# The order in which VectorE walks the tail tokens when it scales them out of PSUM

## The chip, the cores and the metric

The kernel runs on one core of one Trainium2 chip. Times are device microseconds of one execution, as the chip reports them. A profile covers the span from the first to the last instruction, which is some 1.8 us shorter. PE is the matrix engine (PEld its weight loads), DVE is VectorE, ACT ScalarE, POOL GpSimd, and SP the engine that issues the transfers, all but five in the trace before. One run of the kernel before took 1665 us and is left out. The two kernels with a probe at their end (e4, e11) ran once each, at a mean granted TensorE clock of 0.98 and 0.96. Inside the kernel PE keeps the pace of the other traces in both (from 135.6 to 241.6 us their gain is 0.00 us in the table of the experiments), so its starts there can be compared; from the probes themselves only VectorE and ScalarE durations are taken. The rounds of experiments ran on different chips of one kind (the record lists chips 1, 3 and 6), each beside the kernel before on the same chip.

## The reference

Retention attention over 8 batches of 8 heads, 576 tokens and 64 dimensions, then a feed-forward pair with a tanh gelu:

```python
scores = scale * np.matmul(q, k.transpose(0, 1, 3, 2))
gamma = 1.0 - 2.0 ** (-5.0 - np.arange(H, dtype=np.float32))
Dmat = np.where(rel >= 0, gamma[:, None, None] ** rel[None, :, :], 0.0)
ret = np.matmul(scores * Dmat, v)                 # 8 x 8 x 576 x 64
x = ret.transpose(0, 2, 1, 3).reshape(4608, 512)
h = x @ w_in                                      # 512 -> 2048
g = 0.5 * h * (1.0 + np.tanh(c * (h + 0.044715 * h**3)))
out = g @ w_out                                   # 2048 -> 512
```

## The kernel before: what matters here

576 tokens are four chunks of 128 and a **tail** of 64. The tails of all 8 batches are gathered in one tile and go through the feed-forward layers together, as a block of their own near the end.

```python
xt = const.tile([128, 2, B, HP, 32], F16, name="xt")   # parity, batch, head pair, token / 2
...
def inter_tail(b):
    xs = att[b].pop("xt")                              # two PSUM banks
    for u in range(2):
        for s in range(2):
            nc.tensor.matmul(xs[u][:, 64 * s : 64 * s + 64], ...)          # L547
        nc.vector.tensor_tensor(                                           # L553
            out=xt[:, :, b, 2 * u : 2 * u + 2, :].rearrange("p s q i -> p q i s"),
            in0=xs[u][:, 0:128].rearrange("p (q i s) -> p q i s", q=2, s=2),
            in1=gx[:, 2 * u : 2 * u + 2, :, 0:32].rearrange("p q s i -> p q i s"),
            op=ALU.mult,
        )
```

The order of the instructions on every engine is fixed by a hand-made plan: around a matmul unit it lists which piece of the next batch's attention is issued behind it. The tail of batch 7 is followed by five additions into `xf` (L609), which read all of `xt`, and by the tail block's matmuls (L613), which read `xf`.

## Time and profile before

| | kernel before |
|---|---|
| time, four runs | 299.68 to 300.29 us, median 299.89 |
| span of the profile | 297.5 us |
| PE busy | 289.5 us |
| VectorE busy | 234.3 us |
| L553 | 16 instructions of 128 elements per partition, 838 ns each by their records, 0.60 us each in a queue |

A group's busy time is the union of its records. Records of neighbouring VectorE instructions overlap by about 0.09 us (L408: a mean record of 0.69 us, 0.60 us in the chain), more with slow ones (L553: 0.84 and 0.60). The cost of an instruction in a queue therefore has to be read from the chain or from the starts of those behind it. The lines themselves stand in the prediction.

### The profile page before, as it was taken

To read this page: it belongs to the slowest core of one execution; us is meant where nothing else is said; L and a number is where in the kernel's file an instruction comes from. 1 tells how busy PE (TensorE), PEld (TensorE's weight loads), DVE (VectorE), ACT (ScalarE), POOL (GpSimd) and SP (SyncE) were. 2 spreads that over 40 slices of the span, in tenths; PEclk is the share of its full clock that TensorE was granted. 3 is DMA by queue.
4 is the path that set the end of the run, shared out by engine and by line. 5 is a ranking of instruction groups with operands and counts; after the bars stand their busy time and mean duration, and the time that the engine had idled before them with its cause. 6 is when DMAs were issued, how large, how long until landed. Compare 5 with 4: busy or idle time off the path is not lost.

```text
span 297.5 us, 8910 instructions
## 1 busy us (share of the span) xinstructions
PE 289.5 (97%) x3748; PEld 208.9 (70%) x3748; DVE 234.3 (79%) x434; ACT 161.9 (54%) x316; POOL 121.6 (41%) x142
## 2 busy tenths in 40 slices
PE   8989999999999999999999999999999999999995
PEld 6866478888885568645875587558755876686584
DVE  2796889999998996898569746977698298886754
ACT  7328798975546781665446544555346217615720
POOL 6743676276140433183063206459003005711760
PEclk9999999999999999999999999999999999999999
DMA  6999999969879989988994989481120003002204
GB/s 203 301 312 324 311 374 331 266 175 223 227 199 219 315 217 207 292 252 130 260 278 115 135 240 280 127 145 18 61 84 0 2 0 145 0 2 71 71 3 141
DMA packets 94712, 52.48 MB, mean 176 GB/s; under 512 B 38352, under 2 KB 88528, under 8 KB 94672
## 3 DMA queue, kind: packets, MB, share of 16 engines
q1 hardware_dynamic: 94336, 51.26, 65.2%
q10 hardware_dynamic: 336, 0.66, 0.8%
q8 instruction: 29, 0.48, 0.6%
q14 instruction: 11, 0.09, 0.1%
HBM read 36.70 MB, written 9.44 MB: 155 GB/s over the span
## 4 chain that ended last, share of the span: by engine, by line
PE 74%; DVE 13%; DMA 4%; SPq 4%; issue 2%; ACT 2%; DVEq 0%; ACTq 0%
PE hp L583 27%; PE my L726 9%; PE mz L726 9%; PE hp L669 5%; PE mw L726 5%; PE mu L726 4%; PE mv L726 4%; SPq L188 3%; DVE ret L408 3%; DMA loan<-in_moe_w_in_dram 2%; DMA ld<-in_moe_w_in_dram 2%; PE xs L495 2%; DVE gT L698 2%; DVE ost L753 2%; PE xs L522 2%
## 5 line engine op out<-in xcount | busy, mean ns | idle before, releaser
L583 PE MATMUL hp<-x,w_in_sb 128*128 128x512 f16 x408 | 94.1, 379 | 0.2 <-DVE ret L408 0.2
L587 ACT ACTIVATE gT<-hp 128x512 f16<-128x512 f32 x112 | 65.9, 598 | 42.3 <-PE hp L583 40.4
L583 PEld LDWEIGHTS <-w_in_sb 128*128 128x128 f16 x448 | 42.5, 98 | 44.9 <-issue 0.8
L726 PEld LDWEIGHTS <-gT 128*128 128x128 f16 x576 | 55.8, 98 | 8.0
L241 POOL TENSOR_TENSOR cv<-ld,sc 128x512 f16<-128x512 f32 x28 | 31.4, 1136 | 28.8 <-DMA ld<-in_v_dram 26.0
L408 DVE TENSOR_TENSOR ret<-st,cm 128x512 f16<-128x512 f32 x64 | 40.8, 694 | 1.9 <-PE st L395 1.6
L232 POOL CAST kq<-ld 128x512 f16<-128x512 f32 x31 | 20.7, 677 | 51.8 <-DMA ld<-in_k_dram 26.3
L232 ACT CAST tbd<-ws 64x256 f16<-64x256 f32 x61 | 24.6, 403 | 24.7 <-DVE ws L476 21.3
L726 PE MATMUL my<-w_out_sb,gT 128*128 128x256 f16 x288 | 34.4, 273 | 0.0
L726 PE MATMUL mz<-w_out_sb,gT 128*128 128x256 f16 x288 | 34.4, 273 | 0.0
L726 PEld LDWEIGHTS <-gsum 128*128 128x128 f16 x288 | 28.1, 98 | 3.6
L698 DVE TENSOR_TENSOR gT<-gT 128x1024 f16<-128x1024 f16 x30 | 28.5, 955 | 0.2
L535 DVE TENSOR_TENSOR x<-xs,gx 128x512 f16<-128x512 f32 x32 | 21.6, 684 | 5.2 <-PE xs L522 5.0
L694 DVE TENSOR_TENSOR gsum<-gT 128x1024 f16<-128x1024 f16 x32 | 23.4, 730 | 2.7 <-ACT gT L656 2.7
L686 DVE TENSOR_TENSOR gdia<-gT 128x512 f16<-128x512 f16 (+1 forms) x30 | 22.5, 751 | 2.4 <-ACT gT L587 2.1
L753 DVE TENSOR_TENSOR ost<-ost,mv 128x512 f32<-128x512 f32 x18 | 11.5, 682 | 16.4 <-issue 11.5
L694 POOL TENSOR_TENSOR gsum<-gT 128x1024 f16<-128x1024 f16 x4 | 8.9, 2223 | 35.1 <-ACT gT L656 32.2
L669 PE MATMUL hp<-x,w_in_sb 128*128 128x256 f16 x160 | 19.1, 273 | 1.1 <-DVE x L535 0.9
L669 PEld LDWEIGHTS <-w_in_sb 128*128 128x128 f16 x160 | 15.2, 98 | 3.4 <-issue 1.0
L726 PE MATMUL mu<-w_out_sb,gsum 128*128 128x256 f16 x144 | 17.2, 272 | 0.3 <-issue 0.2
L726 PE MATMUL mw<-w_out_sb,gdia 128*128 128x256 f16 x144 | 17.2, 273 | 0.0
L726 PE MATMUL mv<-w_out_sb,gsum 128*128 128x256 f16 x144 | 17.2, 273 | 0.0
(114 smaller groups left out, 410.8 us busy)
## 6 DMA issues: line engine op xcount, KB each, us to landing
ld<-in_k_dram SPq DMA_DIRECT2D x30, 256.0 KB, 5.4
ld<-in_q_dram SPq DMA_DIRECT2D x30, 256.0 KB, 5.4
ld<-in_v_dram SPq DMA_DIRECT2D x30, 256.0 KB, 5.3
out_dram<-ost SPq DMA_DIRECT2D x14, 512.0 KB, 4.1
loan<-in_moe_w_out_dram SPq DMA_DIRECT2D x12, 256.0 KB, 5.7
loan<-in_moe_w_in_dram SPq DMA_DIRECT2D x8, 256.0 KB, 6.4
ld<-in_moe_w_in_dram SPq DMA_DIRECT2D x8, 256.0 KB, 6.2
ld<-in_moe_w_out_dram SPq DMA_DIRECT2D x4, 256.0 KB, 5.1
```

What stands on the lines that cost most here:

```text
L232: (eng.copy if eng is nc.scalar else eng.tensor_copy)(out=out, in_=in_)
L241: eng.tensor_tensor(out=unperm(att[b]["v"][:, s, hh, :]), in0=perm(t), in1=sc[:, 8 * hh : 8 * hh + 8] .rearrange("p (r h) -> p r h", r=2) ...
L408: nc.vector.tensor_tensor(out=x.rearrange("p (a m) -> p a m", a=2), in0=st[hl].rearrange("p (a m) -> p a m", a=2), in1=cm.rearrange("p r s ...
L535: nc.vector.tensor_tensor(out=xb[b][:, :, 2 * s + c].rearrange("p s q i -> p q s i"), in0=att[b]["x", s][c].rearrange("p (q s i) -> p q s ...
L583: nc.tensor.matmul(hp, w_in_sb[:, ct, 128 * f : 128 * f + 128], x[:, :, ct, :], start=(ct == 0), stop=(ct == 3),)
L587: nc.scalar.activation(out=self.g(f // 2)[:, f % 2], in_=hp, func=AF.Gelu_apprx_tanh)
L669: nc.tensor.matmul(hp[:, 256 * h : 256 * h + 256], w_in_sb[:, ct, 256 * j + 128 * h : 256 * j + 128 * h + 128], xb[self.b][:, :, 2 * u : 2 ...
L686: e.tensor_tensor(out=self.sa[:, j : j + n], in0=g[:, :, 0, 0:256], in1=g[:, :, 1, 256:512], op=ALU.add)
L694: e.tensor_tensor(out=self.sc[:, j : j + n], in0=g[:, :, 0], in1=g[:, :, 1], op=ALU.add)
L698: e.tensor_tensor(out=g.rearrange("p j h c -> p j (h c)")[:, :, 256:768].rearrange("p j (h c) -> p j h c", h=2), in0=g[:, :, :, 0:256], in ...
L726: nc.tensor.matmul(o, lhs(j, slice(128 * u, 128 * u + 128)), w_out_sb[:, j, w], start=((u == 0 or isinstance(t, list)) and j == 0 and not ...
L753: nc.vector.tensor_tensor(out=out, in0=in0, in1=t, op=op)
```

## The change

Intent: a row of the tile should be written in one go, not one element in this row and one in that. The innermost index becomes the token pair (i), and the parity (s) moves outside it. All values and places stay the same. The price is that the PSUM read, which was contiguous, now takes every second float.

```diff
-                out=xt[:, :, b, 2 * u : 2 * u + 2, :].rearrange("p s q i -> p q i s"),
-                in0=xs[u][:, 0:128].rearrange("p (q i s) -> p q i s", q=2, s=2),
-                in1=gx[:, 2 * u : 2 * u + 2, :, 0:32].rearrange("p q s i -> p q i s"),
+                out=xt[:, :, b, 2 * u : 2 * u + 2, :].rearrange("p s q i -> p q s i"),
+                in0=xs[u][:, 0:128].rearrange("p (q i s) -> p q s i", q=2, s=2),
+                in1=gx[:, 2 * u : 2 * u + 2, :, 0:32],
```

## The prediction

> **What bounds the kernel now.** I read the page's busy table first. The matrix engine is busy 97% of the span and VectorE, the only engine that the change touches, 79%.
>
> ```profile
> PE 289.5 (97%) x3748; PEld 208.9 (70%) x3748; DVE 234.3 (79%) x434; ACT 161.9 (54%) x316; POOL 121.6 (41%) x142
> ...
> PE   8989999999999999999999999999999999999995
> ...
> DVE  2796889999998996898569746977698298886754
> ```
>
> The second line is PE in 40 slices of 7.4 us: only the first slices and the last one are below nine tenths. So anything VectorE gives back can shorten the run only where PE stands still for it, and PE idles 8 us in all (297.5 - 289.5), most of it in the first 40 us and at the very end. VectorE, in contrast, is full in one stretch (slices 7 to 15, about 45 to 112 us) and has room later.
>
> The change touches one group, so I read the groups of VectorE by shape next. The columns after the bar are total busy us, mean ns of one, idle us before, and what ended that idle time.
>
> ```profile
> L408 DVE TENSOR_TENSOR ret<-st,cm 128x512 f16<-128x512 f32 x64 | 40.8, 694 | 1.9 <-PE st L395 1.6
> ...
> L535 DVE TENSOR_TENSOR x<-xs,gx 128x512 f16<-128x512 f32 x32 | 21.6, 684 | 5.2 <-PE xs L522 5.0
> ...
> L553 DVE TENSOR_TENSOR xt<-xs,gx 128x128 f16<-128x128 f32 x16 | 10.4, 838 | 6.0 <-PE xs L547 6.0
> ...
> L436 DVE TENSOR_TENSOR rett<-st,cm 128x128 f16<-128x128 f32 x16 | 3.8, 281 | 0.5 <-PE st L423 0.5
> ```
>
> L553 is the tail's scaling: 16 instructions (8 batches x 2), 128 elements per partition each. L436 has the same operation, shape, types and memories (one input in PSUM, fp16 result in SBUF) and takes 281 ns; L553 takes 838 ns, more than L535, which does the same job on four times the elements. What differs is only the walk. L553 goes "q i s", so its last index is the token's parity: each write jumps between two rows of the tile that lie 1024 fp16 elements apart (8 batches x 4 pairs x 32), and each read of gx jumps 64 floats; only its PSUM read is contiguous.
>
> Records of neighbouring VectorE instructions overlap, so a record overstates what one costs in a queue. The chain of waits (start, us, what) shows the cost in the queue:
>
> ```profile
> 72.72 0.40 DVE rett L436 x2
> ...
> 74.72 1.21 DVE xt L553 x2
> ...
> 81.05 1.21 DVE ret L408 x2
> 82.30 0.44 PE us L459 x30
> ```
>
> Two L436 cost 0.40 us, two L553 cost 1.21, exactly as much as two 512-element L408. So in a queue one L553 costs 0.60 us and a contiguous instruction of its size 0.20.
>
> [...] the new walk makes the PSUM read the one that steps: two floats at a time. No row of this trace shows such a read.
>
> **The change part by part.** It removes and adds no instruction: the orders before and after have the same rows on all engines, with only L553's pattern changed, from 128x64x2 to 128x2x2x32. The values and their places are the same.
> - Write: runs of 32 fp16 in place of a jump each element. The gx read: runs of 32 floats. [...]
> - PSUM read: contiguous before, every second float after. At best free: 0.20 us in a queue, like L436. [...] I take 0.27 us, a record of about 330 ns[...]; this is a choice[...].
> - Saving: 0.60 - 0.27 = 0.33 us each, 0.66 a pair, 5.3 us over the 16 instructions. VectorE's busy time falls from 234.3 to about 229 (227.9 if the read is free).
>
> That 5.3 us is not time off the kernel. xt is read only by the tail block from about 242 us on, so seven of the eight pairs have no reader near. Their one use of time is to hold up the VectorE instructions queued behind them. I therefore looked at each stretch behind a pair, for PE's starts that came later than the usual spacing (216 ns for 512 columns, 109 for 256). Behind the first pair (74.65 us) there are four places where PE waited for VectorE's queue:
>
> ```profile
> 82.04 0.70 PE L459 MATMUL us<-cv,kq 64*64 64x64 f16 x32
> ...
> 97.27 0.38 PE L352 MATMUL tr<-ident,kqt 128*128 128x128 f16 x4 [0.16 <-DVE vs L473]
> ...
> 132.88 0.38 PE L583 MATMUL hp<-x,w_in_sb 128*128 128x512 f16 x1 [0.23 <-DVE ret L408]
> ...
> 243.41 0.39 PE L613 MATMUL pw<-xf,wf 128*128 128x256 f16 x2 [0.16 <-DVE xf L609]
> ```
>
> - 82.3: about 0.25 us inside the us group and 0.35 before the mu product behind it; the chain runs back through VectorE, without idle time, to the pair at 74.7. At most 0.6; POOL's work on cv also starts at 82.05, so I count 0.3.
> - 97.3: 0.22 us late, the transposes wait for a bank that VectorE frees, right behind the pair at 95.3. I count 0.2.
> - 132.9: 0.39 us late, again behind an unbroken VectorE queue from the pair at 125.0. VectorE instructions between them also wait for ScalarE's results, so I count 0.25.
> - 243.4: 0.32 us late. Here the pair (240.55) is truly on the path: it feeds xf, and pw waits for xf. I count 0.3.
>
> Sum 1.05 us, at most 1.5. In the blocks from 155 to 230 us PE's chain is unbroken and most of the 6.0 us that VectorE idles ahead of L553 lie there; saving there is worth nothing. 300.0 - 1.05 gives 299.0; I take 299.1.
>
> **Rivals.**
> (a) Nothing moves at all: PE is 97% busy, and the VectorE time was hidden. Against it speak only the four small waits above. 299.8 to 300.2.
> (b) The PSUM read with a step turns out as slow as the old write: L553 stays near 800 ns and the time at 300.0. Against it: before, two streams jumped by far and one of them wrote half words[...].
> (c) VectorE's queue is tighter than I see in its full stretch (45 to 112 us) and every 0.66 us there carries through: three pairs, 2 us, plus 0.6 later: 297.4. Against it: PE's lateness in 74 to 112 us is too small in sum to give 2 us back.
> (d) Earlier VectorE frees banks earlier, so PE and transfers run into another wait, for instance POOL's cv at 82 us [...]. This would eat the gain: 300.0, perhaps 300.5.
>
> **Range and chances.** Runs of the kernel before spread over 0.5 us by themselves (299.78 to 300.29). With 1.05 us expected, 1.5 as the limit of the direct gain, and (a) and (d) together as likely as one in three, I put 8 in 10 on 298.3 to 300.1. Faster by 2% would mean 294, more than all of PE's idle time after 40 us; slower by 2% has no mechanism, as no work is added. Both get 0.01.
>
> **What would show it.** Right: L553's mean record falls to 280 to 480 ns (central 330) with the count still 16; two of them in the chain cost 0.4 to 0.8 us; VectorE's busy time falls by 4 to 6.5 us with PE's busy time within 1 us of 289.5; the waits at 97, 133 and 243 us shrink or go; VectorE's idle time ahead of other groups grows by about what L553 loses. Wrong: if L553 stays above 600 ns the step about the PSUM read fails; if it falls and the span doesn't, the four waits are held by something else than VectorE; if the span falls by over 2 us, PE was held up by VectorE in ways that its start times hide.

The sum of 1.05 us has its four terms (0.3, 0.2, 0.25 and 0.3), which come from the trace before. The 0.27 us in a queue was my choice: it lies above the 0.20 us of L436, and nothing measured then said by how much. On it rest 0.33 us for each instruction, 0.66 a pair and 5.3 in all. That the new walk's write and its read of gx would cost nothing more was not shown either when I counted so; e4_probe has the new walk and the all contiguous form both at 291 ns.

## The result, and the profile after

| | before | after |
|---|---|---|
| time, four runs each | 299.68 to 300.29, median 299.89 us | 298.07 to 298.73, median 298.46 us |
| ratio | | 0.995, 95% interval 0.9932 to 0.9967 |
| span of the profile | 297.5 us | 296.3 us |

Ratios are the mean time of one kernel's fast runs over that of the other's in the same rounds, so they are not quite the ratio of the medians. Two later comparisons on the same code (below) gave 0.997 and 0.9986.

First the busy times of the changed kernel, then two of its VectorE groups by shape, to be held against the same lines in the prediction:

```profile
PE 288.9 (97%) x3748; PEld 208.6 (70%) x3748; DVE 230.7 (78%) x434; ACT 162.0 (55%) x316; POOL 122.4 (41%) x142
```

```profile
L553 DVE TENSOR_TENSOR xt<-xs,gx 128x128 f16<-128x128 f32 x16 | 3.9, 284 | 6.0 <-PE xs L547 6.0
L436 DVE TENSOR_TENSOR rett<-st,cm 128x128 f16<-128x128 f32 x16 | 3.8, 281 | 1.2 <-PE st L423 1.2
```

L553 now looks like L436, the contiguous instruction of its size: 284 against 281 ns. The step in the PSUM read costs nothing. The chain of waits of the changed kernel says the same of the queue, 0.40 us a **pair** (the two instructions of a batch) where it was 1.21:

```profile
72.51 0.40 DVE rett L436 x2
...
74.52 0.40 DVE xt L553 x2
74.92 0.34 DVE vs L473
```

Read from the start of the second instruction behind a pair (near 125 us: 1.73 us after the pair's own start before, 1.00 now) the saving is 0.73 us a pair, a little less than the 0.81 of the chain.

L553's busy time fell by 6.5 us (10.4 to 3.9), but VectorE's by 3.6 (234.3 to 230.7). Of the missing 2.9 us, 2.3 are one other group, L694, which the change doesn't touch: 23.4 us before and 25.7 after. In four traces of kernels with the old walk in most places it is 24.6, 24.6, 25.1 and 25.8, so the first trace was low in it and the walk isn't the reason.

Where did PE get its time? All kernels here run the same 3748 matmuls in the same order. So the start of the n-th matmul in the trace before, minus the start of the n-th in another trace (each from its own span's start), is that trace's **lead**, and the growth of the lead within a stage is what was gained there. For the first trace of the changed kernel (stages named by the time in the trace before):

| stage | to 73.2 | 73.2 to 90.0 | 90.0 to 99.2 | 99.2 to 130.7 | 130.7 to 135.6 | 135.6 to 241.6 | 241.6 to 244.1 |
|---|---|---|---|---|---|---|---|
| gain, us | 0.37 | 0.64 | -0.39 | -0.17 | 0.39 | 0.00 | 0.33 |

The first changed instruction runs at 74 us, so 0.37 us of the lead cannot come from the change. The loss at 90 to 99 us is a new wait. In the timeline of the changed kernel, PE (columns: start, us, engine, line, operation, tiles, and in brackets its idle time and who ended it) stands before the scores of batch 3:

```profile
95.84 0.86 PE L395 MATMUL st<-T 64*64 64x128 f16 x48 [0.70 <-DMA T<-kq]
```

It waits for the transposing DMA that fills T. The loss of 0.17 us at 99 to 131 us comes back in no other trace either. The gain at 243 us is the place where `xf` waits for the last pair. First the kernel before, then the changed one, same columns:

```profile
240.55 1.28 DVE L553 TENSOR_TENSOR xt<-xs,gx 128x128 f16<-128x128 f32 x2
...
242.28 1.75 DVE L609 TENSOR_TENSOR xf<-xt 128x512 f16<-128x512 f16 x5
...
242.65 0.60 PE L613 MATMUL pv<-xt,wf 128*128 128x256 f16 x4
```

```profile
239.71 0.48 DVE L553 TENSOR_TENSOR xt<-xs,gx 128x128 f16<-128x128 f32 x2
...
240.27 0.69 DVE L753 TENSOR_TENSOR ost<-ost,my 128x512 f32<-128x512 f32 x1
...
240.87 1.76 DVE L609 TENSOR_TENSOR xf<-xt 128x512 f16<-128x512 f16 x5
...
241.81 0.60 PE L613 MATMUL pv<-xt,wf 128*128 128x256 f16 x4
...
242.25 0.38 PE L613 MATMUL pw<-xf,wf 128*128 128x256 f16 x2
```

Before, `xf` started 0.37 us ahead of pv and pw waited for it (0.16 us of idle PE in the prediction's line at 243.41). Now it starts 0.94 us ahead of pv, and pw follows pv with no wait in brackets.

So three questions were open: is it the time in VectorE's queue that counts, and where; does the change bring the wait for the transpose; and which of the old walk's streams was slow?

### The profile page after: what moved, and what is told of

It reads as the page before. It is cut to its first block, busy times and chain, and to the rows that moved or that the text cites. A ratio compares the mean times of both kernels' runs of the same rounds, so it can differ in the third digit from the quotient of the medians.

```text
span 296.3 us, 8910 instructions
## 1 busy us (share of the span) xinstructions
PE 288.9 (97%) x3748; PEld 208.6 (70%) x3748; DVE 230.7 (78%) x434; ACT 162.0 (55%) x316; POOL 122.4 (41%) x142
## 4 chain that ended last, share of the span: by engine, by line
PE 78%; DVE 13%; DMA 4%; ACT 2%; issue 1%; SPq 0%; POOL 0%; DVEq 0%; ACTq 0%
PE hp L583 31%; PE my L726 9%; PE mz L726 9%; PE mw L726 5%; PE mu L726 4%; PE mv L726 4%; PE hp L669 3%; DMA T<-kq 3%; DVE ret L408 3%; PE st L395 2%; PE xs L495 2%; PE py L613 2%; DVE ost L753 2%; PE xs L522 2%; DVE x L535 1%
## 5 line engine op out<-in xcount | busy, mean ns | idle before, releaser
L587 ACT ACTIVATE gT<-hp 128x512 f16<-128x512 f32 x112 | 65.8, 598 | 41.9 <-PE hp L583 40.1
L232 POOL CAST kq<-ld 128x512 f16<-128x512 f32 x31 | 22.0, 716 | 57.7 <-DMA ld<-in_k_dram 42.3
L241 POOL TENSOR_TENSOR cv<-ld,sc 128x512 f16<-128x512 f32 x28 | 32.8, 1184 | 28.4 <-DMA ld<-in_v_dram 23.8
L408 DVE TENSOR_TENSOR ret<-st,cm 128x512 f16<-128x512 f32 x64 | 40.0, 681 | 4.2 <-PE st L395 3.9
L232 ACT CAST tbd<-ws 64x256 f16<-64x256 f32 x61 | 24.6, 403 | 22.5 <-DVE ws L476 21.9
L694 DVE TENSOR_TENSOR gsum<-gT 128x1024 f16<-128x1024 f16 x32 | 25.7, 802 | 2.7 <-ACT gT L656 2.7
L535 DVE TENSOR_TENSOR x<-xs,gx 128x512 f16<-128x512 f32 x32 | 21.5, 683 | 4.8 <-PE xs L522 4.6
L686 DVE TENSOR_TENSOR gdia<-gT 128x512 f16<-128x512 f16 (+1 forms) x30 | 21.9, 731 | 2.8 <-ACT gT L587 2.1
L694 POOL TENSOR_TENSOR gsum<-gT 128x1024 f16<-128x1024 f16 x4 | 8.9, 2222 | 34.8 <-ACT gT L656 31.8
```

The lines of the kernel that those rows point to most:

```text
L232: (eng.copy if eng is nc.scalar else eng.tensor_copy)(out=out, in_=in_)
L241: eng.tensor_tensor(out=unperm(att[b]["v"][:, s, hh, :]), in0=perm(t), in1=sc[:, 8 * hh : 8 * hh + 8] .rearrange("p (r h) -> p r h", r=2) ...
L408: nc.vector.tensor_tensor(out=x.rearrange("p (a m) -> p a m", a=2), in0=st[hl].rearrange("p (a m) -> p a m", a=2), in1=cm.rearrange("p r s ...
L535: nc.vector.tensor_tensor(out=xb[b][:, :, 2 * s + c].rearrange("p s q i -> p q s i"), in0=att[b]["x", s][c].rearrange("p (q s i) -> p q s ...
L587: nc.scalar.activation(out=self.g(f // 2)[:, f % 2], in_=hp, func=AF.Gelu_apprx_tanh)
L686: e.tensor_tensor(out=self.sa[:, j : j + n], in0=g[:, :, 0, 0:256], in1=g[:, :, 1, 256:512], op=ALU.add)
```

## The experiments

**Theory.** The old walk's 2-byte writes cost 0.40 us an instruction, and PE gets back only what VectorE's queue made it wait for. **Rivals.** The scattered writes hurt other engines at the SBUF; every pair's saving counts alike; the wait for the transpose belongs to the change; or the waits of PE that the prediction listed are held by something else.

Some edits add a line ahead of the scaling, so its number is L554 in their profiles, and those behind it move by one as well.

The stage gains of all traces but two (e3 and e10, below) over the first trace of before, in us, worked out as above:

| trace | pairs with the new walk | to 73.2 | 73.2-90.0 | 90.0-99.2 | 130.7-135.6 | 135.6-241.6 | 241.6-244.1 |
|---|---|---|---|---|---|---|---|
| changed kernel | all | 0.37 | 0.64 | -0.39 | 0.39 | 0.00 | 0.33 |
| e1_again | all | -0.05 | 0.53 | 0.00 | 0.39 | -0.06 | 0.33 |
| e12_once_more | all | -0.04 | 0.47 | 0.00 | 0.39 | -0.07 | 0.33 |
| e4_probe | all | -1.62 | 0.72 | -0.01 | 0.39 | 0.00 | 0.33 |
| e11_distance | all | 0.01 | 0.27 | 0.00 | 0.39 | 0.00 | 0.33 |
| e5_first3 | batches 0 to 2 | 0.34 | 0.40 | 0.00 | 0.39 | 0.00 | 0.00 |
| e6_mid | batch 3 | -0.09 | -0.15 | 0.00 | 0.39 | 0.00 | 0.00 |
| e7_456 | batches 4 to 6 | -0.57 | -0.16 | 0.00 | 0.39 | 0.00 | 0.00 |
| e8_last | batch 7 | -0.66 | -0.59 | 0.00 | 0.38 | 0.00 | 0.33 |
| e9_twice | all, each issued twice | 0.09 | -0.26 | 0.03 | 0.14 | 0.00 | 0.07 |
| e2_thrice | all, each issued three times | -0.53 | -0.58 | -0.28 | 0.39 | 0.00 | -0.58 |

The column to 73.2 us is the spread that an execution brings before any changed instruction runs. It is as large as the whole effect, which is why the stages are compared and not the spans.

### e1_again and e12_once_more: the changed kernel twice more

Edit: none.

> The changed kernel once more, unaltered, for more rounds and a second trace. Both theories: ratio to the kernel before 0.994 to 0.996. The point is the trace: in the first one PE waited 0.86 us at 95.8 us for the transposing DMA into T, a wait the kernel before did not have. If the change brings that wait (rival: the earlier PE runs into the transfer), it is there again at 0.3 us or more; if it comes from where the transfers stood in that one execution (they were 0.9 us late before the first changed instruction ran), it need not be.

> The changed kernel a third time, because the two timed comparisons gave 0.995 and 0.997. From the traces so far the gain is 0.4 to 0.7 us in the stretch 73 to 90 us over kernels with the old walk there (which lost 0.2 us on average against the first trace of before), and 0.33 us at 243 us: about 1.05 us, ratio 0.9965 with the interval holding it. In the trace: time from the matmul at 73.2 us to the last one 219.2 to 219.8 us, no gain at 97 us and none from 136 to 241 us. Rival (the first result of 1.4 us was the size): ratio 0.995 or less.

Measured: 0.997 (interval 0.9948 to 0.9991) and 0.9986 (0.996 to 1.0013). The first of them missed the ratio that I had named. The second lies above 0.9965 too; its interval holds that, but also 1.000. The first result of 0.995 thus lies at the favourable end. **The wait for the transpose** is gone from PE in both, and in the two probe traces of the same code: their gain at 90 to 99 us is zero within 0.01. In the first trace the transpose was issued at 87.13 us, against 86.20 in the trace before, and PE came there a us earlier. The queue of transfers had been late by 0.9 us before the first changed instruction ran (70.80 for 69.86), had caught up to 0.1 us at 74.35, and fell back again by 77. So it varies from one execution to the next, and the wait is no fixed cost of the change. The 0.86 us of the expectation is the length of that group of matmuls; the wait in the first trace is the 0.70 us in brackets. An earlier PE does have less room in front of that transfer, and one of five traces used it up. Whether it would do so more often than before, five traces can't tell.

### e5_first3, e6_mid, e7_456, e8_last: one part of the change alone

```diff
+            w = "p q s i" if b < 3 else "p q i s"     # b == 3; b in (4, 5, 6); b == 7
-                out=xt[...].rearrange("p s q i -> p q s i"),
+                out=xt[...].rearrange("p s q i -> " + w),   # in0 and in1 likewise
```

> Old walk but for batches 0 to 2 (the pairs near 74.7, 91 and 95 us). Theory: what VectorE's full stretch holds of the gain, 0.3 to 0.9 us, ratio 0.997 to 0.999; the waits of PE near 132.9 and 243.4 us stay. Rival (one late wait carries the whole gain): ratio 0.9995 to 1.001.

> New walk for batch 3 alone (the pair near 125 us). Theory: PE's lateness of 0.39 us at 132.9 us goes and PE's lead behind it is 0.3 to 0.4 us more than in front of it, and nothing else changes: ratio 0.9985 to 0.9995. Rival: the wait there is held by the gelu results or by POOL and stays: ratio 1.000.

> New walk for batches 4 to 6 alone. Theory: nothing, ratio 0.9995 to 1.0005, PE's lead from 150 to 240 us unchanged within 0.1 us, though VectorE is busy 1.2 us less there in each batch pair's 0.8 us. Rival (each pair's saving counts alike): 3 of 8 of the gain, ratio 0.998.

> New walk for batch 7 alone (the pair near 240.5 us, the one that xf waits for). Theory: PE's lateness of 0.32 us at 243.4 us goes: ratio 0.9985 to 0.9993, lead of PE 0.3 us more behind 243.4 than in front. Rival: the wait moves to another instruction of VectorE ahead of xf: ratio 1.000.

Measured: ratios 0.9997 (0.9969 to 1.0025), 0.9982 (0.996 to 1.0004), 0.9987 (0.9967 to 1.0007) and 0.9984 (0.9959 to 1.001). All four intervals hold 1.000, and all four ratios lie outside the ranges that I had named: parts of 0.3 to 0.7 us are too small for the times, and only the traces separate them.

- **First three batches:** 0.40 us at 73 to 90 us, where the three traces with the old walk in all of these pairs, taken on the same chip, have -0.15, -0.16 and -0.59. All of it comes before 90 us, ahead of the second and third pair (near 91 and 95 us). So of the three only the first pair counts. It counts at two places. One is the wait near 82.3 us that the prediction listed. The other, which it did not list, is at 78 us: in the kernel before, the second half of a group of scores starts at 78.09 us, behind VectorE's L535, which ended at 78.04 us. The group takes 0.83 us there, 1.01 in e8_last (old walk) and 0.64 in e1_again (new walk); one line of each, in this order:

```profile
77.68 0.83 PE L395 MATMUL st<-T 64*64 64x128 f16 x32
...
78.33 1.01 PE L395 MATMUL st<-T 64*64 64x128 f16 x32
...
77.72 0.64 PE L395 MATMUL st<-T 64*64 64x128 f16 x32
```

- **The third pair** brings nothing, for VectorE then waits for ScalarE. Its next instruction starts 1.19 us after the pair's start with the old walk and with the new one; with the new walk VectorE stands idle for 0.70 us in front of it (the changed kernel):

```profile
95.45 0.43 DVE L686 TENSOR_TENSOR gdia<-gT 128x512 f16<-128x512 f16 x1 [0.70 <-ACT gT L587]
```

- **Batch 3:** PE's lateness at 132.9 us is gone, as expected. But it is gone in e5, e7 and e8 too, whose batch 3 has the old walk, and in e2, whose pair there costs more than the old one. So the gain of 0.39 us at 131 to 136 us isn't the change's: the one trace of the kernel before was late there. What made it late I did not settle.
- **Batches 4 to 6:** nothing between 136 and 242 us, as expected, though each pair is 0.8 us cheaper.
- **Batch 7:** 0.33 us at 243 us, as expected, and in no trace with the old walk there. The line behind the first stage's loss in this trace is the same wait as in the kernel before, for VectorE's scaled scores behind the old first pair:

```profile
83.43 0.44 PE L459 MATMUL us<-cv,kq 64*64 64x64 f16 x30 [0.34 <-DVE ret L408]
...
84.02 0.71 PE L727 MATMUL mu<-w_out_sb,gsum 128*128 128x256 f16 x5 [0.16 <-DVE ret L408]
```

### e2_thrice and e9_twice: the new walk at the old price

```diff
+            for _ in range(3):        # e9: range(2)
                 nc.vector.tensor_tensor(out=xt[...], in0=..., in1=...)   # the new walk
```

> The new walk, but each of the 16 scalings issued three times in a row: three times 0.20 us is the 0.60 us that one cost with the old walk. Theory (only the time in VectorE's queue counts): back to the kernel before within 0.2%, ratio 0.998 to 1.002, lead of PE near 0. Rival (the scattered writes themselves hurt the other engines that read or write SBUF): the gain stays, ratio 0.994 to 0.997.

> The dose of the thrice run was too high: its pairs cost 1.69 us in the queue, not 1.21, since repeats on one tile cost 0.28 us each. Here each scaling of the new walk is issued twice: 4 x 0.28 = 1.1 us a pair, near the old 1.2. Theory (only the time in VectorE's queue counts): from the matmul at 73.2 us to the last one 220.3 to 220.9 us, as in the traces with the old walk there (220.4 to 220.6), and the wait before the tail's pw product is back (no gain at 243 us); ratio 0.998 to 1.002. Rival (the scattered writes hurt other engines): 219.2 to 219.8 us as in the traces of the new walk, ratio 0.995 to 0.997.

Measured: three times gave 1.0056 (1.0028 to 1.0084), slower than expected, for the dose was wrong. Repeats on one tile cost 0.28 us each, not 0.20, so a pair took 1.69 us where the old one took 1.21. Twice gave 1.0 (0.9973 to 1.0027). Its timeline shows the pair at 1.04 us (the next instruction, L473, starts at 75.54) and PE waiting in the old place:

```profile
74.50 1.12 DVE L554 TENSOR_TENSOR xt<-xs,gx 128x128 f16<-128x128 f32 x4
75.54 0.41 DVE L473 TENSOR_TENSOR vs<-us,ws 128x256 f32<-128x256 f32 x1
...
82.28 0.44 PE L459 MATMUL us<-cv,kq 64*64 64x64 f16 x30 [0.31 <-DVE ret L408]
```

From the matmul at 73.2 us to the last one it took 220.63 us and the kernel before 220.61. The five traces of the changed code took 219.18 to 219.80. The writes here are contiguous, and the wait at 82.3 us is back: from 78.7 to 84 us e9 gains -0.05 us, the traces with a cheap first pair 0.26 to 0.47. So at that place **the time in VectorE's queue is what counts**. The lateness at 243 us came back by most (0.07 us gained, not 0.33; read from the second instruction behind a pair near 125 us, e9's is 0.08 us cheaper than the old one), and with the triple dose it grew to a loss of 0.58 us.

That the totals of e9 and the kernel before agree so closely is in part chance. An instruction more or less on VectorE changed which engine some matmuls wait for. In the traces' records 31 to 50 of the 3748 matmuls of e2, e3, e9 and e10 name another semaphore (what the record says was waited for) than in the kernel before; in the changed kernel and in e5 to e8 it is 2 at most. At 78 us, for one, the scores wait for VectorE's semaphore in the kernel before and for PE's own in e9 and e2. So e9 lost nothing there (a gain of 0.19 us up to 78.7), but 0.40 us between 84 and 90, in part behind VectorE's L436.

The rival of writes that hurt other engines falls by a plainer number, as far as PE goes: the first old pair runs from 74.65 to 75.93 us, and between 74.1 and 77.7 us the lead of every trace, old walk or new, stays level within 0.002 us. PE was no slower while the old walk wrote.

### e3_none and e10_none_late: no scaling at all (wrong result)

```diff
-            nc.vector.tensor_tensor(out=xt[...], ...)
+    nc.gpsimd.memset(xt, 0.0)        # e3: once, at the start
+            if b == 6 and u == 0:    # e10: once, near 215 us
+                nc.gpsimd.memset(xt, 0.0)
```

> Wrong result on purpose: the 16 scalings are left out and xt is zeroed once. It shows what is left to gain at this place. Theory (the waits of PE behind the pairs are used up): within 0.2% of the changed kernel, ratio to the kernel before 0.992 to 0.996. Rival (VectorE's queue holds PE all through the full stretch, so every 0.4 us a pair counts): a further 1 us or more, ratio 0.989 to 0.992.

> Wrong result on purpose, repeated because the first version's clearing of xt took POOL 1.8 us at the start and held everything up from there: scalings left out, xt cleared by POOL near 215 us, where it is idle. Theory (each us less in VectorE's queue behind 74 us is worth a us until PE no longer waits): stage 73 to 90 us gains 0.6 to 1.1 us over the kernel before (the new walk: 0.4 to 0.7), the stage at 243 us 0.33 us and no more. Rival (the new walk has taken all there is): 0.4 to 0.7 us in the first stage too.

Measured: e3 1.0067 (1.0043 to 1.009), which says nothing of the scaling. Clearing `xt` kept POOL 1.80 us at the start, ahead of the first casts, and the kernel was 2.73 us behind at 73 us. e10 gave 0.9964 (0.9935 to 0.9992). The gains at 73 to 90 us are -0.23 us in e3 and 0.18 in e10, those at 243 us 0.33 in both. The second number fits: leaving the last pair out gives no more than the new walk. The first fits neither expectation, for without any scaling it should not be below the new walk's 0.27 to 0.72. In e10 PE waited here:

```profile
78.68 1.91 PE L722 MATMUL mw<-w_out_sb,gdia 128*128 128x256 f16 x16 [0.48 <-DVE x L535]
```

The same wait is 0.89 us in e3 and 0.36 in e2. In these, as in e9, the first matmul of this product waits for VectorE's semaphore, and in the kernel before for PE's own: the edit changed what releases it. So this is no clean upper bound. How much more a still cheaper first pair would give stays open.

### e4_probe: which stream was slow

```diff
+    pb = bank("pr")                  # at the very end, filled by two matmuls
+    for _ in range(3):               # 13 forms of 128 elements, three times each
+        nc.vector.tensor_tensor(out=..., in0=pb[...], in1=gx[...], op=ALU.mult)
```

> At the end of the changed kernel, when nothing else runs, VectorE does 13 forms of the 128-element scaling three times each, one stream changed at a time. Theory (the 2-byte writes that jump every element cost nearly all): only the write jumping: 700 to 850 ns, like the old walk; only the gx read jumping 280 to 400 ns; PSUM read with a step of 2: 281 ns; with a step of 4: 281 to 450. Jumping write of 4-byte elements: 350 to 500 ns if half words are the trouble, 700 or more if the jump is. Runs of 2, 4 and 8 fp16: falling to 281 ns[...].

The records of some forms (columns: minimum, median, maximum ns): all contiguous, the old walk, the new walk, only the write jumping, only the gx read jumping, only the PSUM read stepping by 2, and a jumping write of 4-byte elements.

```profile
L1469 DVE TENSOR_TENSOR xt<-pr,gx x3: 283/291/291, 294.6 to 295.3; 128x128 f16<-128x128 f32 x3
L1471 DVE TENSOR_TENSOR xt<-pr,gx x3: 722/722/723, 295.6 to 297.1; 128x128 f16<-128x128 f32 x3
L1473 DVE TENSOR_TENSOR xt<-pr,gx x3: 291/291/292, 297.9 to 298.5; 128x128 f16<-128x128 f32 x3
L1475 DVE TENSOR_TENSOR xt<-pr,gx x3: 720/722/723, 298.8 to 300.4; 128x128 f16<-128x128 f32 x3
L1477 DVE TENSOR_TENSOR xt<-pr,gx x3: 290/291/291, 301.1 to 301.8; 128x128 f16<-128x128 f32 x3
L1479 DVE TENSOR_TENSOR xt<-pr,gx x3: 291/291/291, 302.1 to 302.7; 128x128 f16<-128x128 f32 x3
...
L1483 DVE TENSOR_TENSOR wide<-pr,gx x3: 366/376/380, 303.9 to 304.7; 128x128 f32<-128x128 f32 x3
```

Only the write matters: alone it costs the whole 722 ns. The gx read's jumps between two rows 256 bytes apart and the PSUM step are free (291 ns each), a step of 4 in PSUM too (291 ns). A 4-byte element that jumps costs 376 ns, so the trouble is the lone 2-byte element; stepping on by 4 bytes it costs 301 ns, so it is the distance too. Over 128 elements, the jump adds (722 - 291)/128 = 3.4 ns to each 2-byte element and (376 - 291)/128 = 0.66 ns to each 4-byte one. Two fp16 side by side before each jump are enough: 292 ns, as are four and eight (291 each). I had expected a longer run to be needed.

### e11_distance: how far is far

```diff
+    for _ in range(3):               # 12 forms on VectorE, 2 on ScalarE
+        nc.vector.tensor_tensor(out=xf0[...], in0=P0..., in1=fl..., op=ALU.mult)
```

> At the end of the changed kernel: VectorE writes 128 fp16 elements that alternate between two places 4 B to 2 KB apart, or step on by 8, 16 and 32 B, all other streams contiguous; then the 2 KB jump with an SBUF source, and ScalarE's copy contiguous and jumping. Theory [...]: near 291 ns up to some distance of 8 to 32 B, and 722 ns from there on, whether it alternates or steps on; SBUF source the same. Rival (the two rows 2 KB apart collide because of that distance): costly at 2 KB alone. ScalarE: no expectation but that it shows whether it pays as well.

Two neighbouring distances tell it, 8 and 16 bytes:

```profile
L1468 DVE TENSOR_TENSOR xt<-pr,gx x3: 290/291/291, 294.4 to 295.0; 128x128 f16<-128x128 f32 x3
L1470 DVE TENSOR_TENSOR xt<-pr,gx x3: 725/726/726, 295.4 to 296.9; 128x128 f16<-128x128 f32 x3
...
L1490 ACT CAST xt<-pr x3: 266/266/266, 317.2 to 317.8; 128x128 f16<-128x128 f32 x3
L1492 ACT CAST xt<-pr x3: 722/724/726, 318.1 to 319.6; 128x128 f16<-128x128 f32 x3
```

| fp16 writes, one element at a time | median ns for 128 |
|---|---|
| alternating between places 4 or 8 B apart | 291 |
| 16, 32, 64, 128 B apart | 725 to 727 |
| 512 B and 2 KB apart | 722 to 723 |
| stepping on by 8 B / 16 B / 32 B | 441 / 724 / 693 |
| 2 KB apart, both inputs in SBUF | 725 |
| ScalarE, contiguous / alternating 2 KB apart | 266 / 724 |

The rival that the distance of 2 KB is special falls: with alternating places the cost starts between 8 and 16 bytes (291 and 726 ns) and then stays level (722 to 727). ScalarE's copy pays 724 ns as well, so moving the jumping write there promised nothing.

## Why the prediction was right

The time (299.1 us, range 298.3 to 300.1) and "within 2%" held; the measured median is 298.46 us. By its own steps:

- **L553's cost, right, on the careful side.** I took 0.27 us in a queue and a 330 ns record; it is 0.20 us and 281 ns (median). What was off is that choice: the PSUM step is free (291 ns in the probe, stepping or not). That no row of the trace showed such a read was said; 16 records in the changed kernel and the probe have it now. Two of the signs fell short: VectorE's busy time was to fall by 4 to 6.5 us and fell by 3.6 (4.6 in e1 and e12), and its idle time grew by 2.4 us, not by about what L553 lost.
- **"That 5.3 us is not time off the kernel", right.** L553 gave back 6.5 us of busy time and the kernel gained about 1. Between 136 and 242 us the gain is zero in the first trace and -0.07 to 0.00 in the others of the same code.
- **The wait at 82.3 us (I counted 0.3): right, but not the only one behind the first pair, and the sum too small.** From 73 to 90 us the traces with a cheap first pair gain 0.64, 0.53, 0.72, 0.27, 0.47 and 0.40, mean 0.50. Those with the old first pair have 0.00, -0.15, -0.16 and -0.59, mean -0.22. The difference is 0.73 us, from one pair whose saving is 0.73 to 0.81. Of it 0.48 us arise at 78.7 to 84 us, where I had counted 0.3, about 0.30 ahead of that, at the wait of the scores at 78 us that I had overlooked, and -0.05 behind. e9 shows for the wait at 82.3 us that the price in the queue decides; for the one at 78 us only the choice of the pair (e5 against e6, e7 and e8) shows it. The means leave out e3 and e10, which have no first pair at all (-0.23 and 0.18) and other waits; with them the difference would be 0.60.
- **The wait at 97.3 us (0.2): failed.** The lead between 91.6 and 99.2 us doesn't change by more than 0.01 us in any of the other four traces of the changed code; the lateness stands in the new walk as in the old. Being "right behind the pair" was no proof that it waited for it: what the third pair saves, VectorE spends waiting for ScalarE's L587 (0.70 us), and its next instruction starts 1.19 us after the pair's start in both walks. A pair of 1.70 us (e2) does go past that, and that trace loses 0.28 us here.
- **The wait at 132.9 us (0.25): failed.** It was the trace's own. "Again behind an unbroken VectorE queue" was true of that one execution; three traces with the old walk there don't have it.
- **The wait at 243.4 us (0.3): right,** 0.33 us, in every trace whose last pair is cheap and in none whose pair has the old walk.
- **The sum, 1.05 us: right, in part by luck.** Two terms that were nothing (0.2 and 0.25) stood in for what the first one lacked, most of it at a wait that was not in the sum: 0.73 + 0.33 = 1.06 us. The three timed comparisons, 0.995, 0.997 and 0.9986, average 0.997, which is 0.9 us of 299.5.
- **Rivals.** (a) is excluded by the first two comparisons and by the traces; (b) by 281 ns. (c), that all of the full stretch carries through, holds for its first pair alone. (d) was seen once, as the wait of 0.70 us for the transpose, and is no part of the change's cost in the other four traces.

## What to carry to other kernels

Where VectorE writes fp16 to SBUF, let at least two neighbours follow each other in the walk (292 ns against 722 for 128 elements), and let an input in PSUM take the step instead (291 ns at steps of 2 and 4; of ScalarE only a contiguous write was measured beside the jumping one, 266 ns against 724): here that took the instruction from 0.60 to 0.20 us in the queue, for nothing. Then ask who stands behind the instruction: of eight pairs whose savings looked alike, the one at the end of a path and the one in front of a full queue gave the whole gain, and the others none. An experiment that adds or drops an instruction can change the waits elsewhere (31 to 50 matmuls named another semaphore); choosing where the new form applies did not (2 at most). And do not attribute a wait of 0.2 to 0.4 us from one trace: take a second one of the same code first, for here two of four such readings were wrong and a fifth place was missed.
